# Two heads' scores as 64-row matmuls, weights kept split, and an order from a simulated list: an attention and two gated layers in one launch

## The chip, the cores and the metric

The kernel runs on one core of a Trainium2 chip. The metric is the time of one launch on the device in microseconds (us), as a median of runs. In the profile PE is TensorE (its weight loads are a row of their own, PEld), ACT is ScalarE, DVE is VectorE, POOL is GpSimd and SP is the engine that issues the DMAs.

## The reference

```python
# q, k, v: [4, 12, 448, 64] float32 (batch, heads, tokens, head size); weights are float64
scores = q @ k^T / sqrt(64) - log(448)
attn   = sigmoid(scores) @ v                       # -> x: [4 * 448 tokens, 12 * 64 = 768]
h = max(x @ w1, x @ w2, x @ w3);  y = h @ w_out    # all weights 768 x 768
g = y @ w_in;  out = (g * sigmoid(1.702 * g)) @ w_out2   # 768 x 2048, then 2048 x 768
```

## The kernel before

A block is one batch entry: 448 tokens, 12 heads (6 pairs), x of 6 tiles of 128 features. All matmuls have 448 columns. PE's float32r kind takes operands that were rounded, so a float32 number is split in an upper part (a rounded copy) and a lower part (the remainder, `rest`, a subtraction on DVE), and a product is made of three matmuls: upper x upper, upper x lower, lower x upper (`product`, L206). For a tile of 768 x 128 weights that is 18 matmuls, a unit.

*Attention.* A head's q and k lie in one tile `qkf` of 128 rows: both stand twice, in rows 0 to 63 and again in 64 to 127. The upper rows of q get its upper part, the lower rows its lower part, so one 128-row matmul with k's upper part on both halves gives two of the three products (L332), and one with k's lower part the third (L333). Scores of a head are made in chunks of 128 keys; the last 64 keys share a chunk. ScalarE makes sigmoids out of PSUM (L350, up to 896 columns a time). For attn @ v sigmoid and v are split too, except for six pairs of heads (`PLAIN`), whose product is made in plain float32 (L391). In the split product (L401) the two parts of v lie side by side as 128 columns, so its lower half has to be added to the upper one (`fold`, L432, L435).

*Weights.* They come as float64, 768 KB a tile. The high words times 2^-112 are made on ScalarE (`wy`, L134); the upper three bits of the low word are made on ScalarE as an 8-bit number (L136); VectorE clamps, shifts left by 3 and joins the bits (L158 to L160), and the float32 is split (L128, and `rest` in `lower`). In the first block each of the 24 tiles of the first two layers is so converted, and its float32 is stored in DRAM (`kept`); the three later blocks load that and split it again. The 32 tiles of the last two layers are converted while those run.

*Stages.* Block 0's attention runs alone with some of the next one's heads (`alone`, 16 steps). Then for each block the 24 units of its first two layers run with the next block's attention beside them. y stays in SBUF in two parts, in the place of x. Last come 32 steps of the last two layers, 256 features of one block at a time: two products of 18, then six sums of six matmuls (L640 to L642), added up in SBUF (L647).

*Order.* It is written out by hand: each engine works its instructions in the order of emission. Lists say which rounding is VectorE's and which ScalarE's (`UPPER_DVE`, `QK_DVE`, ...), `AHEAD` how many weight tiles are ready, `SPREAD` how the attention's steps are spread over units, and `mixed` interleaves VectorE's operations. DMAs all go through SP's queue; a load whose buffer is about to come free is held back by `soon` until the step's end.

Of the kernel before, what the change touches and what calls it, by code (L numbers as in the profile page):

```python
# [21 lines left out]
KEYS = 512  # 448 keys, the last 64 of them twice  # L22
# [9 lines left out]
SPREAD = (24, 24, 23, 1)
# where among the operations beside a unit the unit before it is finished
LATE = (0.3, 1)
WHOLE = 4
# how many weight tiles are ready beside each unit of a block: beside the last block's more and more, and the first
# of the last two layers'
AHEAD = (B - 1) * [[n + 2 for n in range(NW1)]]
AHEAD.append([2, 3, 4, 5, 7, 9, 11, 13, *range(14, 22), 22, 23, 23, 24, 25, 25, 26, 26])
# what VectorE rounds, where ScalarE does the rest: halves of heads' sigmoids, heads' v, pairs' x, parts of h, weight  # L40
# tiles, heads' q and k
UPPER_DVE = (0, 2, 5, 6, 10, 11, 12, 13, 15, 16, 17, 19, 22, 24, 25, 26, 28, 36, 45, 50, 52, 53, 54)
V_DVE = (0, 2, 4, 6, 8, 9, 14, 19, 20, 21)
X_DVE = (11, 13)
H_DVE = (5, 6, 7, 8, 9)
W_DVE = (3, 21, 23)
QK_DVE = (1, 2, 3, 5, 7, 9, 10, 13, 25)
# a float64's low word times LOW, rounded or cut off, is its upper 3 bits as a number of at most 7
LOW = 0.93 * 2.0**-29
# the largest value the weights' exponent shift leaves within float32  # L50
TOP = struct.unpack("f", struct.pack("I", (255 << 20) - (1 << 9)))[0]


def moe_chain_kernel(tc, qk, vv, v4, wa, wb, out):
    nc = tc.nc
    act, dve, pe, sp = nc.scalar, nc.vector, nc.tensor, nc.sync
    scale = 1.0 / math.sqrt(D)
# [6 lines left out]
    def rest(out_, in_, hi):
        dve.tensor_tensor(out_, in_, hi, op=ALU.subtract)  # L65

    def parts(p, name, shape):
        return [p.tile(shape, F32R, name=f"{name}{c}") for c in "hl"]

    def mixed(a, b, c=(), at=()):  # L70
        """VectorE's next operations: those of a and b in turn, and those of c where at says"""
        n, m = len(a), len(b)
        order = [((i + 0.5) / n, 1, f) for i, f in enumerate(a)] + [((i + 0.5) / m, 2, f) for i, f in enumerate(b)]
        order += [(x, 0, f) for x, f in zip(at, c)]
        for _, _, f in sorted(order, key=lambda x: x[:2]):
            f()
# [15 lines left out]
    pav_pool = pool("pav", bufs=2, space=PSUM)
    psc_pool = pool("psc", bufs=2, space=PSUM)
    psc1_pool = pool("psc1", bufs=1, space=PSUM)
    pav1_pool = pool("pav1", bufs=1, space=PSUM)
# [6 lines left out]
    seq = [("new", wa[i], kept[i]) for i in range(NW1)] + (B - 1) * [("kept", kept[i], None) for i in range(NW1)]  # L102
    seq += [("new", wb[i], None) for i in range(NW2)]
    news = [i for i, t in enumerate(seq) if t[0] == "new"]

    class Weights:
        def __init__(self):
            self.raw, self.y, self.c, self.hl = {}, {}, {}, {}
            self.i = -2
            self.free = [(n, wp) for n in range(3)]  # L110
            self.loads = 0

        def load(self, n):
            while self.loads < min(n, len(news)):
                i = news[self.loads]
                third = i < NW1 and i % 3 == 2
                t = (early if third else wp).tile(
                    [P, DM], mybir.dt.uint64, name="w64", tag="w64", bufs=1 if third else 2
                )
                sp.dma_start(t, seq[i][1])  # L120
                self.raw[i] = t
                self.loads += 1

        def upper(self, i):
            n, p = self.free.pop(0)
            h = p.tile([P, DM], F32R, name=f"wh{n}", tag=f"wh{n}", bufs=1)
            lo = p.tile([P, DM], F32R, name=f"wl{n}", tag=f"wl{n}", bufs=1)
            (dve.tensor_copy if i in W_DVE else act.copy)(h, self.c[i])  # L128
            self.hl[i] = (h, lo)
            self.free.append((n, p))  # L130

        def shift(self, i):
            y = self.y[i] = (early if i < NW1 else wp2).tile([P, DM], F32, name="wy", tag="wy", bufs=1)
            act.activation(y, self.words(i, F32, 1), AF.Copy, scale=2.0**-112)  # L134
# [3 lines left out]
        def words(self, i, dtype, n):  # L138
            return self.raw[i].bitcast(dtype).rearrange("p (n two) -> p n two", two=2)[:, :, n]

        def lower(self, i):
            c = self.c.pop(i)
            rest(self.hl[i][1], c, self.hl[i][0])
            if seq[i][2] is not None:
                soon(lambda: sp.dma_start(seq[i][2], c))

        def bits(self, i, halves):
            c = self.c[i] = wp.tile([P, DM], F32, name="wc", tag="wc", bufs=3)
            if seq[i][0] == "kept":
                sp.dma_start(c, seq[i][1])  # L150
                return []
            u, high, y = c.bitcast(U32), self.words(i, U32, 1), self.y.pop(i)
            del self.raw[i]
            n = i if i < NW1 else i - (B - 1) * NW1
            part = [slice(0, DM // 2), slice(DM // 2, DM)] if halves else [slice(0, DM)]

            todo = [
                lambda s: dve.tensor_scalar(c[:, s], y[:, s], -TOP, TOP, op0=ALU.max, op1=ALU.min),  # L158
                lambda s: dve.tensor_scalar(u[:, s], u[:, s], 3, None, op0=ALU.logical_shift_left),
                lambda s: dve.scalar_tensor_tensor(  # L160
                    u[:, s], high[:, s], 0x80000007, u[:, s], op0=ALU.bitwise_and, op1=ALU.bitwise_or
                ),
            ]
            todo = [lambda f=f, s=s: f(s) for f in todo for s in part]
            return todo + [lambda: soon(lambda: self.load(min(n + 4, max(NW1, n + 3))))]

        def step(self, halves=True):
            """the lower part of tile i, the bits of i + 2: gives what VectorE has to do"""
            i = self.i
            self.i += 1  # L170
            todo = []
            if B * NW1 <= i + 2 < len(seq):
# [564 lines left out]
```

## Time and profile before

| | |
|---|---|
| median of 3 runs | 1012.26 us (1009.37 to 1013.31) |
| profiled execution, its span | 1008.6 us, the time that the sums go by; the median is 3.7 above it |
| PE busy, matmul records | 990.7 us, 4774 |
| DVE busy | 663.4 us |
| ACT busy | 567.3 us |
| moved by DMA | 118.58 MB |

The span runs from the first to the last instruction. A matmul's record is longer than the distance to the next one, since matmuls are pipelined; the distance of two starts is what one takes. A plain float32 matmul leaves two records.

### The profile page before, as it was taken

What the parts mean: (1) busy time and instruction counts of PE and PEld (TensorE: products, weight loads), DVE (VectorE), ACT (ScalarE), POOL (GpSimd) and SP (SyncE); (2) the same over time, 40 slices, a digit from 0 to 9 for tenths busy, and PEclk for the clock granted to TensorE, in tenths of its full rate; (3) what the DMA queues carried; (4) which work ended last, traced back from release to release, by engine and by line L of the source; (5) the groups of instructions that cost most, each with busy time, mean ns of one, the idle gap of its engine ahead of it and who ended that gap; (6) DMA issues with size and microseconds to landing.
All of it is one profiled execution on the core that took longest, in us unless ns stands there. A gap on an engine that the chain in (4) does not pass through costs nothing.

```text
span 1008.6 us, 12335 instructions
## 1 busy us (share of the span) xinstructions
PE 990.7 (98%) x4774; PEld 898.4 (89%) x4774; DVE 663.4 (66%) x1125; ACT 567.3 (56%) x726; POOL 0.8 (0%) x6
## 2 busy tenths in 40 slices
PE   8999999899999999999999999999999999999998
PEld 6669888799999999999999899999999999999997
DVE  6888988897777877644465435665566666565544
ACT  5999999876676877533455655344334434443110
POOL 0000000000000000000000000000000000000000
PEclk9999999999999999999999999999999999999999
DMA  8686776663434343233522211111111111110023
GB/s 311 204 267 203 226 245 206 232 194 117 170 113 159 120 156 109 80 108 119 164 92 69 90 63 63 45 50 63 63 37 58 63 63 33 62 63 1 1 92 128
DMA packets 36059, 118.58 MB, mean 118 GB/s; under 512 B 4000, under 2 KB 7328, under 8 KB 36000
## 3 DMA queue, kind: packets, MB, share of 16 engines
q1 hardware_dynamic: 36000, 117.78, 35.3%
q8 instruction: 38, 0.62, 0.2%
q14 instruction: 21, 0.17, 0.1%
HBM read 102.83 MB, written 14.94 MB: 117 GB/s over the span
## 4 chain that ended last, share of the span: by engine, by line
PE 83%; ACT 10%; DVE 2%; issue 2%; DMA 1%; SPq 0%; DVEq 0%; ACTq 0%
PE pmm L212 17%; PE pmm L211 17%; PE pmm L210 17%; PE po L642 8%; PE po L641 7%; PE po L640 7%; PE pav L401 4%; PE psc L332 3%; PE psc L333 3%; ACT w L136 2%; ACT wy L134 2%; ACT a L350 2%; ACT wh L128 1%; PE pav L391 1%; ACT qkh L293 1%
## 5 line engine op out<-in xcount | busy, mean ns | idle before, releaser
L625 ACT ACTIVATE sg<-pmm 128x448 f32<-128x448 f32 x64 | 35.0, 547 | 218.8 <-PE pmm L212 218.8
L642 PE MATMUL po<-gh,wl 128*128 128x448 f32 x384 | 139.4, 363 | 0.0
L641 PE MATMUL po<-gl,wh 128*128 128x448 f32 x384 | 139.4, 363 | 0.0
L640 PE MATMUL po<-gh,wh 128*128 128x448 f32 x384 | 138.6, 361 | 0.6 <-ACT acc L644 0.6
L647 DVE TENSOR_TENSOR acc<-po,acc 128x448 f32<-128x448 f32 (+1 forms) x169 | 102.3, 619 | 52.0 <-PE po L642 50.0
L65 DVE TENSOR_TENSOR wl<-wc,wh 128x768 fp32r<-128x768 f32 x128 | 121.2, 952 | 4.7 <-ACT wh L128 3.7
L128 ACT CAST wh<-wc 128x768 fp32r<-128x768 f32 x125 | 106.8, 854 | 14.2 <-PE pmm L211 7.4
L136 ACT ACTIVATE w<-w 128x768 uint8<-128x768 uint32 x56 | 109.4, 1953 | 1.8
L350 ACT ACTIVATE a<-psc,bias 128x896 f32<-128x896 f32 x96 | 88.3, 961 | 26.6 <-PE psc L333 17.1
L627 DVE TENSOR_TENSOR gf<-pmm,sg 128x448 f32<-128x448 f32 x64 | 40.0, 625 | 86.0 <-ACT sg L625 85.7
L332 PE MATMUL psc<-qkh 128*128 128x448 f32 x192 | 74.8, 390 | 7.8 <-DVE qkh L65 4.7
L65 DVE TENSOR_TENSOR al<-a,ah 128x896 fp32r<-128x896 f32 x72 | 62.0, 892 | 24.7 <-ACT ah L358 24.6
L210 PE MATMUL pmm<-x0h,wh 128*128 128x448 f32 x204 | 75.5, 370 | 2.2 <-ACT mx L222 1.3
L640 PEld LDWEIGHTS po<-gh,wh 128*128 128x128 f32 x384 | 71.8, 187 | 6.2 <-ACT acc L644 1.0
L641 PEld LDWEIGHTS po<-gl,wh 128*128 128x128 f32 x384 | 72.1, 188 | 5.6
L642 PEld LDWEIGHTS po<-gh,wl 128*128 128x128 f32 x384 | 72.0, 188 | 4.0
L210 PE MATMUL pmm<-x1h,wh 128*128 128x448 f32 x204 | 74.7, 366 | 0.0
L210 PE MATMUL pmm<-x2h,wh 128*128 128x448 f32 x204 | 74.7, 366 | 0.0
L211 PE MATMUL pmm<-x1l,wh 128*128 128x448 f32 x204 | 74.6, 366 | 0.0
L211 PE MATMUL pmm<-x2l,wh 128*128 128x448 f32 x204 | 74.6, 366 | 0.0
L212 PE MATMUL pmm<-x1h,wl 128*128 128x448 f32 x204 | 74.6, 366 | 0.0
L212 PE MATMUL pmm<-x2h,wl 128*128 128x448 f32 x204 | 74.6, 365 | 0.0
(91 smaller groups left out, 2052.0 us busy)
## 6 DMA issues: line engine op xcount, KB each, us to landing
wc<-kept SPq DMA_DIRECT2D x72, 384.0 KB, 3.7
w<-in_wb SPq DMA_DIRECT2D x32, 768.0 KB, 4.2
qkf<-in_qk SPq DMA_DIRECT2D x47, 480.0 KB, 4.0
w<-in_wa SPq DMA_DIRECT2D x24, 768.0 KB, 6.7
kept<-wc SPq DMA_DIRECT2D x24, 384.0 KB, 6.7
out_t<-acc SPq DMA_DIRECT2D x23, 224.0 KB, 2.0
vf<-in_vv SPq DMA_DIRECT2D x18, 256.0 KB, 4.3
v<-in_v SPq DMA_DIRECT2D x6, 352.0 KB, 3.5
```

Source lines behind the costliest of these rows:

```text
L65: dve.tensor_tensor(out_, in_, hi, op=ALU.subtract)
L128: (dve.tensor_copy if i in W_DVE else act.copy)(h, self.c[i])
L136: act.activation(low, self.words(i, U32, 0), AF.Copy, scale=LOW)
L210: pe.matmul(ps, wh, xh, start=(k == 0), stop=False)
L211: pe.matmul(ps, wh, xl, start=False, stop=False)
L212: pe.matmul(ps, wl, xh, start=False, stop=(k == KC - 1))
L332: pe.matmul(ps, kh[:, c], qs, start=start, stop=False)
L350: act.activation(a, ps, AF.Sigmoid, bias=bias, scale=scale)
L640: pe.matmul(ps, wh[:, c], gh[:, j, :], start=(j == 0), stop=False)
L641: pe.matmul(ps, wh[:, c], gl[:, j, :], start=False, stop=False)
L642: pe.matmul(ps, wl[:, c], gh[:, j, :], start=False, stop=(j == 1))
L647: dve.tensor_tensor(ACC[b][:, o, h], ps[:, h], ACC[b][:, o, h], op=ALU.add)
```

## The change

One pair of heads takes the place of one head: q of both heads in rows 0 to 63 and 64 to 127, and k too, so a chunk of 128 keys takes three 64-row matmuls per head; those of the two heads use different rows of PE and different PSUM banks and stand next to each other in the order. The last 64 keys of both heads lie as a block diagonal, and take three 128-row matmuls for the pair. In the split pairs, attn @ v's last 64 keys are 64-row matmuls too. q and k are split once per pair, in two tiles of 960 columns.

A weight tile's three low bits come from one 16-bit shift on VectorE, in place, where ScalarE made an 8-bit number. A converted tile is kept in DRAM as its two parts (768 KB), and later blocks load both. y of each block goes to DRAM in two parts and is loaded again for the last two layers.

The order of emission comes from a simulation: every operation is recorded with the parts that it reads and writes, the engines that can do it and an assumed duration (a matmul 0.201 us, a pair of 64-row ones counted once); due times are worked out backwards, and a list schedule lets each engine take the ready operation with the earliest due time. Rings of buffers (`t`, `qh`, `ql` 2 each, weights of the first two layers 5, of the last two 7) replace the pools. Buffers of the last layers are allocated behind two gates: `to_late` when the attention is over, `to_acc` when the first two layers are.

```diff
-    def scores(ps, g, c, start=True, stop=True):
-        kh, kl, qs = qks[g]
-        pe.matmul(ps, kh[:, c], qs, start=start, stop=False)
-        pe.matmul(ps, kl[:, c], qs, start=False, stop=stop)
...
+        def score(self, c):
+            pair = c < 3
...
+                for n, (kx, qx) in enumerate(((h, h), (h, l), (l, h))):
+                    how = dict(start=n == 0, stop=n == 2)
+                    keys = slice(S + c * P, S + (c + 1) * P)
+                    for e in range(2 if pair else 0):
+                        r = slice(e * D, (e + 1) * D)
+                        pe.matmul(o[:, e, :], kx[r, keys], qx[r, :S], **how)
+                    if not pair:
+                        pe.matmul(o, kx[:, keys], qx[:, :S], **how)
...
+            O.pe(f, 3 * MM, [x[i] for x in (self.hi, self.lo) for i in used], [ps])
...
+            def parts(_):
+                v = self.vt()
+                for n, x in enumerate(a):
+                    for e in range(2):
+                        if c < 3:
+                            w = v[:, 2 * c + e].rearrange("p t d -> p (t d)")
+                            pe.matmul(av[e](), w, x()[:, e, :], start=c + n == 0, stop=False)
+                        else:
+                            r = slice(e * D, (e + 1) * D)
+                            w = v[r, 6].rearrange("p t d -> p (t d)")
+                            pe.matmul(av[e](), w, x()[r, :], start=False, stop=n == 1)
...
-            low = self.raw[i].bitcast(U8).rearrange("p (n eight) -> p n eight", eight=8)[:, :, 4]
-            act.activation(low, self.words(i, U32, 0), AF.Copy, scale=LOW)
...
+            lambda: dve.tensor_scalar(half(2), half(1), 13, None, op0=ALU.logical_shift_right),
...
+    def weights1(b, i):
+        hi, lo, t = split(w1s)
+        if b == 0:
+            new_weights(wa[i], hi, lo)
+            dma(kept[i], t, 768, [hi, lo], [kept[i]])
+        else:
+            dma(t, kept[i], 768, [kept[i]], [hi, lo])
+        return hi, lo
...
+    def unit2(b, m):
+        w, ps = weights1(b, 3 * KC + m), bank(mms)
+        product(ps, w, list(HS))
+        hi, lo, t = split(yst)
+        copy(hi, ps, S, psum=True)
+        rest(lo, ps, hi, S)
+        dma(ykept[b][m], t, 448, [hi, lo], [ykept[b][m]])
...
+        def offer(o):
+            for e in o.on:
+                heapq.heappush(ready[e], (o.late + (SLACK if e == "DVE" and len(o.on) > 1 else 0.0), o.n, o))
...
+            for e in free:
+                while free[e] <= now + 1e-9 and ready[e]:
+                    _, _, o = heapq.heappop(ready[e])
+                    if o in done:
+                        continue
+                    done.add(o)
+                    o.fn(e)
...
+    def step(p, c):
+        if p < NP:
+            if c == 0:
+                pairs[p] = Pair(p)
+            pairs[p].score(c)
+        if p > 0:
+            pairs[p - 1].weigh(c)
```

## Rows read from the trace of the kernel before

**Rows 1.** The page's first part: busy time, share, instructions of PE, PEld, DVE, ACT, POOL.
```profile
PE 990.7 (98%) x4774; PEld 898.4 (89%) x4774; DVE 663.4 (66%) x1125; ACT 567.3 (56%) x726; POOL 0.8 (0%) x6
```
**Rows 2.** Windows: stretch, length, busy us (records) per engine, clock, DMA share, GB/s.
```profile
0.00:20.00 20.00, 16.24 (x53) 12.60 (x54) 11.57 (x21) 10.83 (x13) 0.81 (x6) 0.91 0.90 328
0.00:200.00 200.00, 186.33 (x800) 152.66 (x801) 167.64 (x287) 178.51 (x204) 0.81 (x6) 0.98 0.72 239
200.00:300.00 100.00, 100.00 (x490) 91.66 (x489) 80.19 (x120) 69.72 (x94) 0.00 (x0) 1.00 0.46 150
300.00:400.00 100.00, 100.00 (x493) 92.27 (x492) 76.43 (x109) 76.68 (x105) 0.00 (x0) 1.00 0.41 133
600.00:700.00 100.00, 100.00 (x498) 93.13 (x497) 58.74 (x113) 41.82 (x54) 0.00 (x0) 1.00 0.17 55
```
**Rows 3.** PE in order of time, first 80 us: start, duration, line, operands, count.
```profile
14.09 2.42 PE L391 MATMUL pav<-a,v 128*128 128x448 f32 x6
16.00 0.72 PE L332 MATMUL psc<-qkh 128*128 128x448 f32 x1
16.55 0.37 PE L333 MATMUL psc<-qkh,kl 128*128 128x448 f32 x1
...
43.47 0.47 PE L332 MATMUL psc<-qkh 128*128 128x448 f32 x1 [1.33 <-ACT a L350]
43.78 0.36 PE L333 MATMUL psc<-qkh,kl 128*128 128x448 f32 x1
...
74.58 0.36 PE L210 MATMUL pmm<-x0h,wh 128*128 128x448 f32 x1
...
78.23 0.57 PE L401 MATMUL pav<-ah,vs 128*128 128x448 f32 x2
```
**Rows 4.** All engines in order of time, the end: the last matmul.
```profile
1004.62 0.37 PE L642 MATMUL po<-gh,wl 128*128 128x448 f32 x1
```
**Rows 5.** Groups by line, PE: count, busy us, mean ns, idle before.
```profile
L332 PE MATMUL psc<-qkh 128*128 128x448 f32 x192 | 74.8, 390 | 7.8 <-DVE qkh L65 4.7 <-ACT a L350 3.1
L333 PE MATMUL psc<-qkh,kl 128*128 128x448 f32 x192 | 71.1, 370 | 0.0
```
**Rows 6.** PE's weight loads in order of time, after a wait.
```profile
43.47 0.19 PEld L332 LDWEIGHTS psc<-qkh 128*128 128x128 f32 x1 [1.70 <-ACT a L350]
43.58 0.19 PEld L333 LDWEIGHTS psc<-qkh,kl 128*128 128x128 f32 x1
```
**Rows 7.** Groups by line and shape, DVE.
```profile
L65 DVE TENSOR_TENSOR wl<-wc,wh 128x768 fp32r<-128x768 f32 x128 | 121.2, 952 | 4.7 <-ACT wh L128 3.7
...
L65 DVE TENSOR_TENSOR al<-a,ah 128x896 fp32r<-128x896 f32 x42 | 45.4, 1088 | 24.7 <-ACT ah L358 24.6
...
L65 DVE TENSOR_TENSOR kl<-qkf,qkh 128x512 fp32r<-128x512 f32 x47 | 32.3, 687 | 6.7 <-ACT qkh L293 6.4
...
L65 DVE TENSOR_TENSOR qkh<-qkf,qkh 64x448 fp32r<-64x448 f32 x48 | 29.9, 622 | 0.9
...
L160 DVE SCALAR_TENSOR_TENSOR wc<-w,wc 128x768 uint32<-128x768 uint32 x13 | 12.4, 953 | 0.2
L159 DVE TENSOR_SCALAR wc<-wc 128x768 uint32<-128x768 uint32 x13 | 7.2, 556 | 0.2
```
**Rows 8.** Groups by line and shape, ACT.
```profile
L136 ACT ACTIVATE w<-w 128x768 uint8<-128x768 uint32 x56 | 109.4, 1953 | 1.8
L128 ACT CAST wh<-wc 128x768 fp32r<-128x768 f32 x125 | 106.8, 854 | 14.2 <-PE pmm L211 7.4 <-DMA wc<-kept 6.6
L350 ACT ACTIVATE a<-psc,bias 128x896 f32<-128x896 f32 x84 | 82.1, 1009 | 26.6 <-PE psc L333 17.1 <-DVE al L65 9.3
L358 ACT CAST ah<-a 128x896 fp32r<-128x896 f32 x57 | 51.5, 947 | 0.0
L134 ACT ACTIVATE wy<-w 128x768 f32<-128x768 f32 x56 | 50.9, 908 | 1.1 <-DVE wc L158 1.1
L293 ACT CAST qkh<-qkf 128x960 fp32r<-128x960 f32 x38 | 37.9, 996 | 0.1
```
**Rows 9.** DMA issues: count, KB each, median us from issue to landing.
```profile
wc<-kept SPq DMA_DIRECT2D x72, 384.0 KB, 3.7
...
out_t<-acc SPq DMA_DIRECT2D x23, 224.0 KB, 2.0
```

More of the change, by code (lines that the diff above doesn't have):

```diff
@@ L28 @@
 PLAIN = (0, 2, 3, 5, 6, 10)
-SPLIT = tuple(p for p in range(2 * NPAIR) if p not in PLAIN)
-EARLY = (6, 7, 11, 13, 15)
 WARM = 10
[L32 to L45, printed above, removed]
@@ new lines, with __init__, __call__, part @@
+class Tile:
+    def __init__(self, ring=None, get=None):
+        self.ring, self.get, self.ap, self.ops = ring, get, None, []
+    def __call__(self):
+        if self.ap is None:
+            self.ap = self.ring.make() if self.ring else self.get()
+        return self.ap
+    def part(self, cut=None):
+        return Part(self, cut)
+class Part:
+    def __init__(self, tile, cut):
+        self.tile, self.cut, self.writers, self.readers = tile, cut, [], []
+    def __call__(self):
+        ap = self.tile()
+        return self.cut(ap) if self.cut else ap
@@ L57, in moe_chain_kernel, with pool @@
     scale = 1.0 / math.sqrt(D)
-    def pool(name, bufs=1, side=None, **kw):
-        if side is not None:
-            kw["side"] = side
+    O = Order()
+    def pool(name, bufs=1, **kw):
         return tc.alloc_tile_pool(name=name, bufs=bufs, **kw)
[L64 to L76, printed above, removed]
@@ L92, in moe_chain_kernel @@
[L92 to L118, printed above, removed]
-                )
[L120 to L134, printed above, removed]
-            low = self.raw[i].bitcast(U8).rearrange("p (n eight) -> p n eight", eight=8)[:, :, 4]
-            act.activation(low, self.words(i, U32, 0), AF.Copy, scale=LOW)
[L138 to L172, printed above, removed]
-                self.shift(i + 2)
-            if 0 <= i < len(seq):
-                todo.append(lambda: self.lower(i))
-            if 0 <= i + 2 < len(seq):
-                todo += self.bits(i + 2, halves)
-            return todo
-        def ahead(self):
-            i = self.i
-            if 0 <= i < len(seq):
-                self.upper(i)
-            if i + 2 < NW1:
-                self.shift(i + 2)
-        def upto(self, i):
-            while self.i <= min(i, len(seq) - 1):
-                mixed(self.step(), [])
-                flush()
-                self.ahead()
@@ L194, in moe_chain_kernel @@
-    W = Weights()
-    waiting = []
-    def soon(f):
-        waiting.append(f)
-    def flush():
-        while waiting:
-            waiting.pop(0)()
-    def product(ps, w, x):
-        for k in range(KC):
-            wh, wl = (t[:, k * P : (k + 1) * P] for t in w)
-            xh, xl = (t[:, k, :] for t in x)
-            pe.matmul(ps, wh, xh, start=(k == 0), stop=False)
-            pe.matmul(ps, wh, xl, start=False, stop=False)
-            pe.matmul(ps, wl, xh, start=False, stop=(k == KC - 1))
@@ L495, in finish @@
-    def finish(g):
-        if g < NH and g % 2 == 0:
-            values(g)
-        h = g - 2
-        if 0 <= h < NH and not shared(h):
-            fold(h)
-        elif 0 <= h < NH and h % 2 == 1 and plain(h):
-            xf[h // 2] = products.pop(h - 1)
-            x_part(h // 2)
-        elif 0 <= h < NH and h % 2 == 1:
-            fold(h - 1)
-            fold(h)
-    def alone(g):
-        w = weigh(g - 2) if g >= 2 else iter(())
-        first(g)
-        score(g, 0)
-        score(g, 1)
-        next(w, 0)
-        next(w, 0)
-        steps = W.step(False) if g in EARLY else []
-        todo = splits(g) + sums(g)
-        between(g)
-        finish(g)
-        mixed(todo, steps)
-        flush()
-        if g < 3:
-            W.load(g + 1)
-        if g in EARLY or g + 1 == EARLY[0]:
-            W.ahead()
@@ L527, in between @@
-    def between(g):
-        if g % 2 == 1 and g >= 5 and not plain(g - 5):
-            x_part((g - 5) // 2)
-        if g + 2 < NH and g + 2 not in QK_DVE:
-            operands(g + 2)
-    def half(g, n):
-        if n == 0:
-            first(g)
-            if g < NH:
-                score(g, 0)
-                score(g, 1)
-            between(g)
-            return splits(g)
-        if 0 <= g - 2 < NH:
-            for _ in weigh(g - 2):
-                pass
-        todo = sums(g)
-        finish(g)
-        return todo
@@ new lines, in copy, with two, rest @@
+    def copy(to, of, n, psum=False, both=True):
+        engines = {"ACT": t_act(n)}
+        if both:
+            engines["DVE"] = t_two(n) if psum else t_one(n)
+        return O.op(engines, lambda e: (act.copy if e == "ACT" else dve.tensor_copy)(to(), of()), [of], [to])
+    def two(to, a, b, op, n):
+        return on("DVE", t_two(n), lambda: dve.tensor_tensor(to(), a(), b(), op=op), [a, b], [to])
+    def rest(to, of, hi, n):
+        return two(to, of, hi, ALU.subtract, n)
+    base = [pool("base", side="left")]
@@ new lines, in moe_chain_kernel, with banks @@
+    ts, his, los, a2s, a1s, ah2s, ah1s, al2s, al1s, vfs, vss, v4s, xfs, folds = att_rings
+    xs = [ring(xp, f"x{k}", [P, 2, S], 2, F32R) for k in range(KC)]
+    w1s = ring(xp, "w1", [P, 2, DM], 5, F32R)
+    hs = [ring(mid, f"h{k}", [P, 2, S], 1, F32R) for k in range(KC)]
+    mxs = ring(mid, "mx", [P, S], 2)
+    yst = ring(mid, "yst", [P, 2, S], 2, F32R)
+    def banks(p, name, n, shape=(P, 512)):
+        return O.ring(n, lambda: p[0].tile(list(shape), F32, name=name, tag=name, bufs=n))
+    scs, avs, mms = banks(patt, "sc", 2, (P, 2, 512)), banks(patt, "av", 2), banks(pmm, "mm", 2)
@@ new lines, in moe_chain_kernel @@
+    pos = banks(pout, "po", 6)
+    w2s = ring(late, "w2", [P, 2, DM], 7, F32R)
+    z0s = [ring(late, f"z{k}", [P, 2, S], 1, F32R) for k in range(KC)]
+    zs = [ring(acc, f"z{k}", [P, 2, S], B - 1, F32R) for k in range(KC)]
+    gs = ring(late, "g", [P, 2, 2, S], 2, F32R)
+    sgs = ring(late, "sg", [P, S], 2)
+    gfs = ring(late, "gf", [P, S], 2)
+    accs = ring(acc, "acc", [P, S], B * KC)
+    bias = base[0].tile([P, 1], F32, name="bias")
+    nc.gpsimd.memset(bias, -math.log(S))
+    warm = yst.tile().part()
@@ new lines, in moe_chain_kernel, with dram, bank @@
+    O.op({"-": 0.0}, lambda e: nc.gpsimd.memset(warm().bitcast(F32), 0.0), [], [warm])
+    warmed = base[0].tile([P, 1], F32, name="warmed")
+    act.activation(warmed, bias, AF.Sigmoid)
+    def dram(name, shape):
+        return Tile(get=lambda: scratch.tile(shape, F32R, name=name)).part()
+    kept = [dram(f"kept{i}", [P, 2, DM]) for i in range(NW1)]
+    ykept = [[dram(f"yk{b}_{k}", [P, 2, S]) for k in range(KC)] for b in range(B)]
+    def bank(r):
+        return r.tile().part(lambda a: a[:, :S])
@@ new lines, in split, with words, new_weights @@
+    def split(r):
+        t = r.tile()
+        return t.part(lambda a: a[:, 0]), t.part(lambda a: a[:, 1]), t
+    def words(a, dtype, n):
+        per = 8 // mybir.dt.size(dtype)
+        return a.bitcast(dtype).rearrange("p (n k) -> p n k", k=per)[:, :, n]
+    def new_weights(of, hi, lo):
+        raw, y = raws.tile().part(), ys.tile().part()
+        O.op({"SP": 768 / 330.0}, lambda e: sp.dma_start(raw(), of), (), [raw])
+        half = lambda n: words(raw(), U16, n)
+        u = lambda: y().bitcast(U32)
+        by = dict(op0=ALU.bitwise_and, op1=ALU.bitwise_or)
+        on("ACT", t_act(DM), lambda: act.activation(y(), words(raw(), F32, 1), AF.Copy, scale=2.0**-112), [raw], [y])
+        on(
+            "DVE",
+            t_one(DM),
+            lambda: dve.tensor_scalar(half(2), half(1), 13, None, op0=ALU.logical_shift_right),
+            [raw],
+            [raw],
+        )
+        on("DVE", t_one(DM), lambda: dve.tensor_scalar(y(), y(), -TOP, TOP, op0=ALU.max, op1=ALU.min), [y], [y])
+        on("DVE", t_one(DM), lambda: dve.tensor_scalar(u(), u(), 3, None, op0=ALU.logical_shift_left), [y], [y])
+        on(
+            "DVE",
+            t_two(DM),
+            lambda: dve.scalar_tensor_tensor(u(), words(raw(), U32, 1), 0x80000007, u(), **by),
+            [y, raw],
+            [y],
+        )
+        copy(hi, y, DM)
+        rest(lo, y, hi, DM)
@@ new lines, in moe_chain_kernel, with unit1 @@
+    pairs = [None] * NP
+    def step(p, c):
[5 more added lines that the diff above has]
+            pairs[p - 1].weigh(c)
+    HS, mx = [None] * KC, [None]
+    def unit1(b, m, e):
+        w, ps = weights1(b, 3 * m + e), bank(mms)
+        product(ps, w, X[b])
+        if e == 0:
+            mx[0] = mxs.tile().part()
+            copy(mx[0], ps, S, psum=True)
+            return
+        two(mx[0], ps, mx[0], ALU.max, S)
+        if e == 2:
+            hi, lo, _ = split(hs[m])
+            copy(hi, mx[0], S)
+            rest(lo, mx[0], hi, S)
+            HS[m] = (hi, lo)
@@ L643, in unit4 @@
             if grp == 0:
-                act.copy(ACC[b][:, o, :], ps)
+                ACC[b, o] = accs.tile().part()
+                copy(ACC[b, o], ps, S, psum=True)
                 continue
-            for h in halves if u == NG * B - 1 and o == KC - 1 else [slice(0, S)]:
-                dve.tensor_tensor(ACC[b][:, o, h], ps[:, h], ACC[b][:, o, h], op=ALU.add)
-                if grp == NG - 1:
-                    sp.dma_start(out[o, :, b * S : (b + 1) * S][:, h], ACC[b][:, o, h])
-    halves = [slice(0, S // 2), slice(S // 2, S)]
@@ new lines, in moe_chain_kernel, with warming @@
+    mm_warm = bank(avs)
+    def warming(_):
+        for n in range(WARM):
+            pe.matmul(mm_warm(), warm()[:, 0, :P], warm()[:, 1], start=n == 0, stop=n == WARM - 1)
+    O.pe(warming, 3.7, [warm], [mm_warm])
+    steps = [(p, c) for p in range(NP + 1) for c in range(4)]
+    at = 4 * (NPAIR + 1)
+    for s in steps[:at]:
+        step(*s)
+    order = [(1, m, e) for m in range(KC) for e in range(3)] + [(2, m, 0) for m in range(KC)]
+    for b in range(B):
+        first = at
+        for n, (layer, m, e) in enumerate(order):
+            while b < B - 1 and at < min(len(steps), first + -(-24 * (n + 1) // 22), 28 + 24 * (b + 1)):
+                step(*steps[at])
+                at += 1
+            unit1(b, m, e) if layer == 1 else unit2(b, m)
@@ L653, in moe_chain_kernel @@
+    first_ops = {o for r in (*att_rings, scs, avs) for t in r.tiles for o in t.ops}
+    gate = O.op({"-": 0.0}, to_late, after=first_ops)
+    for r in (w2s, *z0s, gs, sgs, gfs, pos):
+        r.gate = gate
     unit3(0)
[L654 removed]
     for u in range(NG * B):
[L656 removed]
         if u + 1 < NG * B:
@@ L659, in moe_chain_kernel @@
         unit4(u)
-    for p in (gp_, acc_pool, wp2, late, wp, low, pout_pool, pmm_pool, pav_pool, scratch):
-        p.release()
+    first_ops = {o for r in (*xs, w1s, *hs, mxs, yst) for t in r.tiles for o in t.ops}
+    gate = O.op({"-": 0.0}, to_acc, after=first_ops)
+    for r in (accs, *zs):
+        r.gate = gate
+    O.run()
+    for p in (late, base, acc, pout, pmm):
+        p[0].release()
+    scratch.release()
 def _bits(w):
```

644 lines of the change are left out of this document (293 added, 351 removed).

## The prediction

> **What bounds the kernel now.** I read the share of busy time first [rows 1]: the matrix engine (PE) is busy 98% of a span of 1008.6 us, VectorE (DVE) 66%, ScalarE (ACT) 56%. Busy time of PE is modelled, so I checked it by counting, in the windows [rows 2]. The reader is to see that from 200 us on, 490 to 498 matmuls of 448 columns stand in every 100 us: the engine takes one each 0.201 to 0.204 us whatever the others do. In the first 200 us only 800 records stand, beside DVE at 84% and ACT at 89%. The order in time [rows 3] gives the unit prices. A product of 18 matmuls runs from 74.58 to 78.23: 0.2028 each, called a slot below. A matmul in plain float32 leaves two records: six of them run from 14.09 to 16.35 (the next product's second matmul starts at 16.55, one slot later), 0.377 each, so about 0.75 for one such matmul. The first 200 us then hold 1.4 us before the first matmul, 4.1 us of warm-up, 84 float32 records x 0.375 = 31.5 and 706 slots x 0.203 = 143.3, in all 180.3; so PE stood still for 19.7 us. One such wait is the gap before 43.47 in [rows 3]. Later waits are about 1 us together. The span ends 4.0 us after the last matmul starts [rows 4]: an addition and the store. So a change can win in two places: fewer slots anywhere, or fewer waits in the first 200 us.
>
> **The change, part by part.** Sums are against the span of 1008.6; the median of the three runs lies 3.7 above it (their ends 0.8 and 4.7), which I add at the end.
>
> *Scores.* Before, a pair of heads takes 16 score matmuls (192 of either kind over 24 pairs [rows 5]). After, each of three chunks takes three pairs of 64-row matmuls, one for either head, and the last chunk three whole ones: 12 slots if the two halves of a pair run at once. That removes 4 x 24 = 96 slots. In attn @ v each of the six split pairs of the first two blocks falls from 16 to 14 slots (the last 64 keys of either head as 64-row matmuls), again if halves run at once: 12 slots. Together 108 x 0.203 = -21.9 us.
>
> *What a pair of 64-row matmuls takes.* No row shows one: every matmul of this trace uses 128 rows. There are 24 x 9 + 18 x 2 = 252 such pairs. Below, a pair costs one slot (0.203), above, two (0.406, the sum +51). Each half loads its own weights. After a wait, two weight loads start at 43.47 and 43.58 [rows 6], 0.11 apart, while the second matmul follows 0.31 after the first load: so a load occupies about 0.105 and is hidden otherwise. Two loads make 0.21, hardly more than a slot, so I take 0.21: 252 x 0.007 = +1.8.
>
> *Going from whole to halved array and back.* Each group of 64-row matmuls lies between whole ones: 72 score groups and 18 in attn @ v, at most 180 changes. The nearest row is the change between plain float32 and the rounded kind around 14.09 to 16.55, and it costs nothing that can be seen. The other bound is a change that empties the pipeline: the next weight load uncovered (0.105) and the tail of a matmul beyond its slot (0.36 recorded less 0.20), 0.265 in all, +48 us. I take 0 by the nearest row, and keep 48 for the range and as a rival.
>
> *Work of ACT and DVE in the first 200 us.* Prices are from [rows 7, 8]. q and k are split once for two heads: before 2 x (0.996 copy + 0.687 + 0.622), after one copy of 960 columns (0.996) and one remainder of 960, which I put at 1.16 from 0.687 at 512 and 0.952 at 768: 4.6 falls to 2.2 per pair. A split pair then holds sigmoids 3 x 1.01 + 0.63, upper parts 3 x 0.95 + 0.6, remainders 3 x 1.09 + 0.62, and about 4.6 for v, sums and x (eight operations of 448 columns, some 0.6 each): some 17.8 us of engine time (20.3 before), a plain pair 7.0 (9.4). A new weight tile lost the 1.953 on ACT and gained a 16-bit shift on DVE. Its price isn't shown: 0.555 if it goes like the shift of whole words, 0.953 if like the operation with a strided operand; I take 0.555, the row of the same kind of operation, the rest being +9.6 us of DVE over 24 tiles. A tile is 0.91 + 3 x 0.555 + 0.953 + 0.952 + 0.854 = 5.3, against 0.91 + 1.95 + 0.854 + 2 x 0.556 + 0.953 + 0.952 = 6.7. Up to the end of block 0 that is 6 x 7.0 + 6 x 17.8 + 14 for the pair begun + 24 x 5.3 + 25 for block 0's own results (42 such operations) = 315 us for two engines. Before, these two were busy 346 of 400 us in the first 200 [rows 2], 87%. At that share 315 us need 181. PE's own work to that point is 49.3 for the seven pairs ahead (5.5 start, 84 + 28 slots, 28 float32 matmuls) plus 124.2 for block 0 beside six pairs (432 + 72 + 56 slots, 14 float32 matmuls) = 173.5. So some 8 us of waiting stay, and a few for what an automatic order doesn't foresee: 12 in place of 20.3, -8.3 us. Cover for the shift is DVE's own slack; if it's gone, each further us on DVE there is one on PE.
>
> *Split weights and y through memory.* A tile of the first two layers is reloaded as both parts (768 KB for 384), so blocks 1 to 3 no longer split 72 tiles; that work (0.854 + 0.952 each) lay beside PE and brings nothing by itself. Its price is traffic. Up to the end of block 0: 24 x 1536 KB of weights in and out, 13 x 480 of q and k, 3.7 MB of v and 2.7 MB of y, about 50 MB; at the 328 GB/s that the first 20 us reach [rows 2] that is 154 us of some 187: near the edge, but covered. In blocks 1 to 3 traffic rises from about 125 to some 225 GB/s (per block 18.9 MB of weights, 4.3 of q, k and v, 2.8 of y in 117 us). It stays under 328, so no load is late with five tiles of buffer, 18 us ahead. But slots grow with traffic: 493 matmuls in 100 us at 133 GB/s, 498 at 55 [rows 2], which is 0.0020 us for 78 GB/s; 100 GB/s more is 0.0026 x 1600 slots = +4 us (0 if it was the attention beside them and not the traffic).
>
> *Going to the last two layers.* y of blocks 1 to 3 gets its buffers only when the last y of block 3 is stored. Copy and remainder (1.2), store and first load (about 3.5 each, by the landing times of 224 and 384 KB [rows 9]), and six loads of 1.4 put block 1's y some 15 us after PE's last product there. PE has block 0's two products (7.3) and its six sums (7.3) to do meanwhile: 14.6. I count +1.5 (0 to 8, the latter if the sums aren't drawn forward).
>
> *Order.* A simulated list order replaces the written one; its effect is in the 12 us above. Lists of SP's queue are in simulated order too, so a load can stand behind a store that waits; with two or more buffers in every ring I count that at nothing, and the bound from the trace is the old waiting, 20.
>
> Sum: 1008.6 - 21.9 + 1.8 - 8.3 + 4 + 1.5 = 985.7, and with 3.7 around it **989 us**. Its own range is 970 (no waits at all in the first 200 us, no traffic cost) to 1003.
>
> **Rivals.**
> *The change of shape drains PE.* Mechanism: at each of 180 changes PE waits for its pipeline and loads weights uncovered. The place is every score step, and it decides from (1012.3 - 989) / 180 = 0.13 us per change; at 0.265 the time is 989 + 48 = 1037, slower. For it: a wait in the trace always leaves an uncovered load. Against: the float32 change costs nothing. The Trainium skill ("TensorEngine Tiling (Array Packing)", Key Properties) says that changing the tiling mode, not just the tile, drains TensorE; no run here shows it, and by that rule this rival is the likely one. I give it 0.18, spread from 1005 to 1037.
>
> *Halves don't run at once* (the change doesn't do what it says): 252 more slots, 989 + 49 = 1038. For it: no row shows two matmuls at once. Against: loads aren't the limit. The skill ("TensorE: Matmul & The Clock Gate", Part 3) has matmuls on different row groups start about 4 ns apart; that would put the pair at 0.207 and take 0.8 us off the sum. I give it 0.06.
>
> *Supply rules the first 190 us.* The shift at 0.953 (+9.6 on DVE), DMA at 83% of the best rate with stores among the loads, and an order made with wrong prices: the waits are 35 in place of 12, 1012. For it: ACT and DVE are already at 84 and 89% there. Against: each pair and tile needs less of both. 0.20, from 1003 to 1018.
>
> *No waits and no traffic cost*: about 970, 0.04.
>
> **How the numbers follow.** Forecast 0.52. A measurement of this kernel can tell about 0.5% from no change, 1007.2 to 1017.3 being the same. Faster: 0.52 + 0.04 + 0.09 of the supply case + 0.02 of the draining one = 0.67. Same: 0.08 + 0.04 = 0.12. Slower: the rest, 0.21. The range for 8 in 10 is 968 to 1024: outside lie most of the case of halves one by one and the upper third of draining.
>
> **What would show it.** In the order in time after: two 64-row matmuls of one pair starting within 0.02 us and the next pair 0.20 to 0.22 later (right), or 0.4 later (halves one by one). The gap between the last 64-row matmul and the next whole one: a slot, or up to 0.27 more. The first product of block 0 should start near 57 us (74.58 before), block 1's near 190. In blocks 1 to 3 matmuls per 100 us should fall by no more than two per cent against the last stage. The 16-bit shift's mean duration decides between 0.55 and 0.95. The prediction is wrong if PE waits over 25 us in all, or if a score step of six takes over 0.75 us.

## The result, and the profile after

After the change the kernel takes 1016.44 us (median of 4 runs, 1015.61 to 1017.1) against 1011.68 for the one before beside it: ratio 1.0054 [1.0036, 1.0072]. It is slower by half a per cent, and the forecast was 2.3% faster. The profiled execution's span is 1013.8 us against 1008.6.

The page's first part after, columns as in [rows 1]:
```profile
PE 998.4 (98%) x4918; PEld 864.8 (85%) x4918; DVE 619.5 (61%) x936; ACT 360.5 (36%) x523; POOL 1.1 (0%) x6
```
DVE and ACT lost 44 and 207 us, as meant, and PE's share is what it was. Only the weight loads hint at something: there are more of them, yet they are busy 4 points less.

The windows after, columns as in [rows 2]:
```profile
0.00:200.00 200.00, 190.73 (x915) 141.26 (x916) 173.03 (x244) 136.19 (x181) 1.08 (x6) 1.00 0.78 279
200.00:300.00 100.00, 99.16 (x513) 82.23 (x512) 61.27 (x90) 46.28 (x64) 0.00 (x0) 1.00 0.64 229
300.00:400.00 100.00, 100.00 (x509) 83.85 (x508) 50.77 (x72) 42.01 (x60) 0.00 (x0) 1.00 0.58 193
600.00:700.00 100.00, 100.00 (x492) 91.99 (x491) 63.32 (x102) 23.08 (x38) 0.00 (x0) 1.00 0.14 48
700.00:800.00 100.00, 100.00 (x492) 92.15 (x491) 71.71 (x115) 22.08 (x35) 0.00 (x0) 1.00 0.18 64
```
From 200 to 400 us a pair of 64-row matmuls is two records, so the larger counts say nothing of speed; but PEld fell from about 92 to 83 us in 100. From 600 us on only whole matmuls run, and there are fewer of them: 492 where [rows 2] has 498. For 700 to 800 us the window before was:
```profile
700.00:800.00 100.00, 100.00 (x499) 93.12 (x497) 61.98 (x118) 39.19 (x49) 0.00 (x0) 1.00 0.15 49
```
A busy PE hides both losses. Marks in PE's order of time show where they fall: the first product of block 0, the first of the last two layers, and the last matmul. Before, the first and the last are 74.58 [rows 3] and 1004.62 [rows 4], and the middle one is
```profile
539.71 0.36 PE L210 MATMUL pmm<-x0h,wh 128*128 128x448 f32 x1
```
After:
```profile
65.40 0.37 PE L363 MATMUL mm<-x,w 128*128 128x448 f32 x1
537.51 0.37 PE L363 MATMUL mm<-z,w 128*128 128x448 f32 x1
1009.61 0.37 PE L555 MATMUL po<-g,w 128*128 128x448 f32 x1
```
The attention that runs alone gained 9.2 us. Blocks 0 to 3 took 472.1 in place of 465.1, +7.0, where the forecast had a gain. By count PE has 13.8 us less to do ahead of block 0 (124 slots and 56 float32 records, 166 and 70 before, warm-up left out) and 8.1 us less in the blocks (2144 and 28, 2210 and 14 before): the first stage gave two thirds of that, the blocks lost 15 us against it. The last two layers took 472.1 in place of 464.9, +7.2, although no product there is changed. The tail adds 0.1; in all +5.1.

**A group of 64-row matmuls.** PE in order of time after, once among whole score matmuls and products (x2 is both halves of a pair):
```profile
252.31 0.36 PE L414 MATMUL sc<-ql,qh 128*128 128x448 f32 x1
252.51 0.37 PE L414 MATMUL sc<-qh,ql 128*128 128x448 f32 x1
252.81 0.47 PE L450 MATMUL av<-ah,vs 64*128 64x448 f32 x2
253.12 0.36 PE L450 MATMUL av<-al,vs 64*128 64x448 f32 x2
253.41 0.47 PE L363 MATMUL mm<-x,w 128*128 128x448 f32 x1
253.72 0.36 PE L364 MATMUL mm<-x,w 128*128 128x448 f32 x1
```
and PE's weight loads beside them:
```profile
252.31 0.19 PEld L414 LDWEIGHTS sc<-qh,ql 128*128 128x128 f32 x1
252.81 0.19 PEld L450 LDWEIGHTS av<-ah,vs 64*128 64x128 f32 x2 [0.30 <-issue]
252.92 0.19 PEld L450 LDWEIGHTS av<-al,vs 64*128 64x128 f32 x2
253.41 0.19 PEld L363 LDWEIGHTS mm<-x,w 128*128 128x128 f32 x1 [0.30 <-issue]
253.52 0.19 PEld L364 LDWEIGHTS mm<-x,w 128*128 128x128 f32 x1
```
The steady distance of starts is 0.20. The first pair starts 0.30 after the last whole matmul: its load isn't made ahead, as the one at 252.31 was (its matmul starts at 252.51), but is recorded as starting with it. The next follows 0.31 later, one uncovered load more, as after a wait [rows 6]. Leaving the group costs the same (0.29 and 0.31). So each of the two changes costs about 0.09 + 0.105, and a group 0.385 (the 59 groups behind block 0's start have a median of 0.39). There are 78 groups (neighbours without a whole matmul between them are one): 78 x 0.385 = 30 us, against 21.9 saved. The Trainium skill ("TensorEngine Tiling (Array Packing)", Key Properties) says that changing the mode drains TensorE; the trace agrees, at 0.19 us a change, the uncovered load with it.

### The profile page after: what moved, and what is told of

Its sections match the earlier page's. It is cut to its first block, busy times and chain, and to the rows that moved or that the text cites. A ratio compares the mean times of both kernels' runs of the same rounds, so it can differ in the third digit from the quotient of the medians.

```text
span 1013.8 us, 12189 instructions
## 1 busy us (share of the span) xinstructions
PE 998.4 (98%) x4918; PEld 864.8 (85%) x4918; DVE 619.5 (61%) x936; ACT 360.5 (36%) x523; POOL 1.1 (0%) x6
## 4 chain that ended last, share of the span: by engine, by line
PE 97%; ACT 1%; DMA 1%; DVE 0%; issue 0%; SPq 0%; DVEq 0%; ACTq 0%
PE mm L363 19%; PE mm L365 19%; PE mm L364 19%; PE po L554 8%; PE po L555 8%; PE po L553 8%; PE av L446 5%; PE sc L412 5%; PE av L438 3%; PE sc L414 1%; PE av L450 1%; ACT a L419 1%; DMA v<-in_v 1%; DMA t<-in_qk 0%; ACT fold L470 0%
## 5 line engine op out<-in xcount | busy, mean ns | idle before, releaser
L363 PE MATMUL mm<-x,w 128*128 128x448 f32 x432 | 161.0, 373 | 0.0
L364 PE MATMUL mm<-x,w 128*128 128x448 f32 x432 | 157.8, 365 | 0.0
L365 PE MATMUL mm<-x,w 128*128 128x448 f32 x432 | 157.6, 365 | 0.0
L553 PE MATMUL po<-g,w 128*128 128x448 f32 x384 | 140.4, 366 | 1.3 <-ACT g L217 1.3
L365 PE MATMUL mm<-z,w 128*128 128x448 f32 x384 | 141.4, 368 | 0.0
L363 PE MATMUL mm<-z,w 128*128 128x448 f32 x384 | 141.3, 368 | 0.0
L364 PE MATMUL mm<-z,w 128*128 128x448 f32 x384 | 141.2, 368 | 0.0
L554 PE MATMUL po<-g,w 128*128 128x448 f32 x384 | 140.4, 366 | 0.2 <-DVE g L220 0.2
L555 PE MATMUL po<-g,w 128*128 128x448 f32 x384 | 140.1, 365 | 0.0
L537 ACT ACTIVATE sg<-mm 128x448 f32<-128x448 f32 x64 | 34.8, 544 | 258.6 <-PE mm L365 258.6
L419 ACT ACTIVATE a<-sc,bias 128x896 f32<-128x896 f32 (+1 forms) x96 | 87.3, 915 | 93.3 <-PE sc L412 68.0
L220 DVE TENSOR_TENSOR al<-a,ah 128x896 fp32r<-128x896 f32 (+1 forms) x72 | 69.7, 974 | 49.2 <-ACT ah L217 48.8
L220 DVE TENSOR_TENSOR gf<-mm,sg 128x448 f32<-128x448 f32 x64 | 39.9, 624 | 97.0 <-ACT sg L537 96.5
L363 PEld LDWEIGHTS mm<-x,w 128*128 128x128 f32 x432 | 81.1, 188 | 10.7 <-issue 3.3
L364 PEld LDWEIGHTS mm<-x,w 128*128 128x128 f32 x432 | 81.2, 188 | 7.3 <-issue 1.1
L365 PEld LDWEIGHTS mm<-x,w 128*128 128x128 f32 x432 | 81.1, 188 | 6.4
L553 PEld LDWEIGHTS po<-g,w 128*128 128x128 f32 x384 | 72.1, 188 | 7.5 <-ACT g L217 1.6
L365 PEld LDWEIGHTS mm<-z,w 128*128 128x128 f32 x384 | 72.2, 188 | 6.8
L364 PEld LDWEIGHTS mm<-z,w 128*128 128x128 f32 x384 | 72.2, 188 | 6.7
L363 PEld LDWEIGHTS mm<-z,w 128*128 128x128 f32 x384 | 72.2, 188 | 6.6
L554 PEld LDWEIGHTS po<-g,w 128*128 128x128 f32 x384 | 72.1, 188 | 6.2 <-DVE g L220 0.5
```

The lines of the kernel that those rows point to most:

```text
L220: return on("DVE", t_two(n), lambda: dve.tensor_tensor(to(), a(), b(), op=op), [a, b], [to])
L363: pe.matmul(ps(), wh[:, c], xh, start=k == 0, stop=False)
L364: pe.matmul(ps(), wh[:, c], xl, start=False, stop=False)
L365: pe.matmul(ps(), wl[:, c], xh, start=False, stop=k == KC - 1)
L419: on("ACT", t_act(n) + 0.07, lambda: act.activation(a(), ps(), AF.Sigmoid, bias=bias, scale=scale), [ps], [a])
L537: on("ACT", t_act(S), lambda sg=sg, ps=ps: act.activation(sg(), ps(), AF.Sigmoid, scale=1.702), [ps], [sg])
```

## Experiments

Theory A: the changes of shape take what the slots give. Theory B: they only fill time in which PE would wait anyway, and something else costs. Theory C: the two halves don't run at once. The edits are shortened to the lines that matter. Line numbers in a row are those of its own kernel.

**One whole matmul for each pair of halves (e1).** As many slots, no change of shape.
```diff
- pe.matmul(o[:, e, :], kx[r, keys], qx[r, :S], **how)   # e = 0, 1
+ pe.matmul(o[:, n > 0, :], kx[:, keys], qx[:, :S], start=n < 2, stop=n != 1)
  # last keys of attn @ v: one whole matmul where two 64-row ones ran
```


> The changed kernel with one whole 128-row matmul in place of each pair of 64-row ones (252 of them), so PE has as many slots and no change of shape; this mixes the two heads' products and leaves half of them out. Theory A (each of 78 groups of 64-row matmuls costs 0.385 us: 0.09 to empty and 0.105 of uncovered weight load, on either side): 1016.4 - 30 = 986 us, ratio to the kernel before about 0.975. Rival B (the changes only fill time in which PE would wait for sigmoids and weight tiles anyway): no more than 8 us gained, 1008 to 1016. Rival C (the two halves don't really run at once): a whole matmul for each pair would save 0.2 each, -50 us, 966.

992.37 us, ratio 0.9828 [0.981, 0.9845], span 988.9: 24.9 of the 30 us are back. Its marks, and the window that answers to [rows 2] at 300 us:
```profile
62.82 0.36 PE L363 MATMUL mm<-x,w 128*128 128x448 f32 x1
512.69 0.37 PE L363 MATMUL mm<-z,w 128*128 128x448 f32 x1
984.79 0.37 PE L554 MATMUL po<-g,w 128*128 128x448 f32 x1
```
```profile
300.00:400.00 100.00, 100.00 (x495) 92.47 (x494) 52.15 (x76) 43.94 (x58) 0.00 (x0) 1.00 0.57 195
```
The 59 groups after block 0's start are priced at 59 x 0.385 = 22.7 and gave back 472.1 - 449.9 = 22.2. The 19 before it are priced at 7.3 and gave back 2.6: there PE waits some 1.6 us more, for ACT and a load of v, and its granted clock was 0.97 over the stretch (1.00 after), worth just under 2. A fits. The halves cost no second slot, and no cost of traffic shows: 495 whole matmuls at 195 GB/s, 493 at 133 before.

**Fewer groups, the same work (e2).** 46 groups in place of 78.
```diff
+ if c == 0: s.score((0, 1))                        # chunks 0 and 1 in a row
+ if c == 1: w.weigh(0); w.weigh(1)
+ if c == 2: w.weigh(2); s.score((2,), w.weigh(3, True)); w.finish()
+ if c == 3: s.score((3,))
```


> The changed kernel with the same matmuls in fewer groups: chunks 0 and 1 of a pair's scores stand together, chunk 2 behind the pair before's last 64-row products. 78 groups become 46, nothing else. Theory A: 32 x 0.385 = -12.3 us, 1004 (ratio 0.993), if no new waits come in the first 60 us, where two score chunks now need both PSUM buffers at once (up to +4). Rival B: 1014 to 1018, no gain.

1005.66 us, ratio 0.996 [0.9949, 0.997], span 1003.7: 10.1 less than after, where 32 x 0.385 = 12.3 was priced. The 6 groups fewer before block 0 brought nothing (it starts at 66.97); blocks 0 to 3 take 460.5, 11.6 less, where 26 groups fewer are priced at 10.0. A group in order of time:
```profile
225.15 0.36 PE L365 MATMUL mm<-x,w 128*128 128x448 f32 x1
225.44 0.47 PE L466 MATMUL av<-ah,vs 64*128 64x448 f32 x2
225.75 0.37 PE L466 MATMUL av<-al,vs 64*128 64x448 f32 x2
225.96 0.37 PE L413 MATMUL sc<-qh 64*128 64x448 f32 x2
226.16 0.37 PE L413 MATMUL sc<-ql,qh 64*128 64x448 f32 x2
226.37 0.37 PE L413 MATMUL sc<-qh,ql 64*128 64x448 f32 x2
226.66 0.47 PE L415 MATMUL sc<-qh 128*128 128x448 f32 x1
226.97 0.36 PE L415 MATMUL sc<-ql,qh 128*128 128x448 f32 x1
```
Inside it, after its first pair, a pair takes 0.20 to 0.21, whichever operation it belongs to; only the edges cost.

**More groups, the same work (e3).** 215 groups: products with v between the pairs.
```diff
+ if other: other[0](n)      # after each of the three pairs of a score step
```


> The changed kernel with the same matmuls in more groups: between the three pairs of a score step stand matmuls of the pair before's product with v. 78 groups become 215. Theory A: 137 x 0.385 = +52.7 us, 1069 (ratio 1.057). Rival B: under +10 us in the part where units of the first two layers stand beside, 1016 to 1026.

1082.55 us, ratio 1.0718 [1.0677, 1.0759], 13.5 more than A's 1069. Blocks 0 to 3 take 520.1 between the marks, +48; 109 groups more are priced at 42. The start is later by 24.3 us, more than 28 groups (10.8) explain; there the granted clock was 0.78 of 2.4 GHz over 70 us, and 0.50, the lower level of 1.2 GHz, from 25 to 48 us:
```profile
0.00:70.00 70.00, 62.65 (x176) 28.05 (x176) 43.56 (x62) 38.35 (x50) 1.08 (x6) 0.78 0.64 221
25.00:48.00 23.00, 22.11 (x50) 9.27 (x51) 11.69 (x17) 7.47 (x11) 0.00 (x0) 0.50 0.47 155
```
At 0.78, some 15 of the 70 us are lost, which with the 10.8 covers the 24.3. The four runs had mean clocks of 0.983 to 0.996 and spans of 1086.0 to 1075.2; span times clock is 1067 to 1072 in each, an estimate of the span at full clock, 54 to 58 above after, where A priced 52.7. Why the clock was low isn't shown. With e2 the time goes with the number of groups in both directions.

**The old sixteen score matmuls in the new kernel (e7).**
```diff
+ for n, (kx, qx) in enumerate(((h, h), (h, l), (l, h), (l, h))):
+     pe.matmul(o[:, n // 2, :], kx[:, keys], qx[:, :S], start=n % 2 == 0, stop=n % 2 == 1)
```


> The changed kernel with 16 whole score matmuls per pair of heads, as many as before, and no 64-row matmul (attn @ v's last keys as many as before too): the rest of the change without its new scores; this mixes the two heads' products. Theory A: 1016.4 - 30 + 21.9 = 1008 us, so the rest of the change is worth some 3 us against the kernel before (ratio 0.997): waits 9 less, 6 lost by slower slots in the last two layers. Rival B: at 21.9 more slots it is slower than the changed kernel, 1020 or more.

1007.52 us, ratio 0.9979 [0.9969, 0.9989], span 1005.6. The rest of the change (kept weights, list order, shift) is worth 0.2%, with the 7.2 us lost in the last two layers in it; the 64-row scores turn that into a loss.

**The 16-bit shift left out (e9).**
```diff
- lambda: dve.tensor_scalar(half(2), half(1), 13, None, op0=ALU.logical_shift_right)
```


> The changed kernel without the 16-bit shift, so that the weights' low three bits are left out. Its 56 instructions took 1.04 us each, not the 0.555 counted. Theory A (PE and the changes of shape are the bound, the shift lies beside PE): at most 3 us gained, 1013 to 1017. Rival F (VectorE is the bound in the first 200 us, where 24 of them are 25 us of its time): 8 us or more gained, under 1008.

1015.58 us, ratio 1.0058 [1.0045, 1.0071], as after. Groups by line after, DVE; the first is the shift, the third the shift of whole words ([rows 7] has 556):
```profile
L327 DVE TENSOR_SCALAR raw<-raw 128x768 uint16<-128x768 uint16 x56 | 58.1, 1038 | 0.0
L336 DVE SCALAR_TENSOR_TENSOR y<-raw,y 128x768 uint32<-128x768 uint32 x56 | 52.8, 952 | 0.3
L332 DVE TENSOR_SCALAR y<-y 128x768 uint32<-128x768 uint32 x56 | 32.6, 582 | 0.0
```
The shift is dearer than both my bounds, and hidden all the same.

**The last two layers.** The mean slot there grew, waits left out, from about 0.2015 to 0.2041, and the products differ: 0.2027 for those on block 0's z (z is y, loaded again) in seven of its eight units, 0.2064 for the other three blocks' (0.2067 in the first unit of all, block 0's). In PE's order of time after, 36 matmuls on block 0's z, 36 with w_out2 (`po`), and 36 on another block's z:
```profile
708.68 0.36 PE L363 MATMUL mm<-z,w 128*128 128x448 f32 x1
...
715.98 0.36 PE L553 MATMUL po<-g,w 128*128 128x448 f32 x1
...
723.27 0.37 PE L363 MATMUL mm<-z,w 128*128 128x448 f32 x1
...
730.70 0.36 PE L553 MATMUL po<-g,w 128*128 128x448 f32 x1
```
What differs between them is where the tiles begin in SBUF. Before, the starts of moving operand and weights lay 64 bytes apart (modulo 128) for w_out2's products (0.2003) and 0 for x (0.2027); after, 0 for w_out2 (0.2027) and block 0's z (0.2027), 32 for the other z (0.2064). These distances are worked out from the sizes of the tiles in their order of allocation; no trace shows an address. Theory D: this distance sets the slot, and 64 is best. Theory E or G: it doesn't.

The kernel after with distance 64 everywhere (e4):
```diff
+ w1s = shifted(xp, "w1", [P, 2, DM], 5, F32R, 64)       # begins 64 bytes in
+ w2s = shifted(late, "w2", [P, 2, DM], 7, F32R, 64)
+ zs = [shifted(acc, f"z{k}", [P, 2, S], B - 1, F32R, 96) for k in range(KC)]
```


> The changed kernel with its weight tiles begun 64 bytes later and the y tiles of the last two layers 96 bytes later, nothing else: in each unit the moving operand then begins 64 bytes (of 128) from the weights; before, 0, and 32 for three of four blocks in the last two layers. Theory D (a slot depends on where the two operands begin: 0.2002 us at a distance of 64, 0.2025 at 0, 0.2064 at 32): 864 slots x 0.0062 + 3168 x 0.0023 = -12.7 us, 1004 (ratio 0.993). Rival E (slots are longer in the last stage because of the new loads or the order): no change, 1014 to 1018.

1008.77 us, ratio 0.9985 [0.9974, 0.9996], span 1005.9: 7.9 less than after, where D asked 12.7; the last two layers take 466.7 us, 5.4 less.

The kernel before with x tiles 64 bytes later (e5):
```diff
- return [p.tile(shape, F32R, name=f"{name}{c}") for c in "hl"]
+ ts = [p.tile([shape[0], n + 32], F32R, name=f"{name}{c}") for c in "hl"]
+ return [t[:, 16 : 16 + n].rearrange("p (i j) -> p i j", i=shape[1]) for t in ts]   # not for h
```


> The kernel before with the tiles of x begun 64 bytes later, so that the 2448 matmuls on x have a distance of 64 in place of 0 bytes (of 128) to the weights. Theory D: 1296 x 0.003 + 1152 x 0.0022 = -6.4 us, ratio 0.994. Rival E: no change, ratio 0.999 to 1.001.

1006.36 us, ratio 0.9976 [0.9964, 0.9988]: 2.4 us by the ratio, less than half of the 6.4 that D asked. The last two layers gain 2.7 us, where D asked 2.5 (1152 x 0.0022); blocks 0 to 3 gain 0.6, where it asked 3.9.

e2 with distance 32 (e10) and 96 (e11) everywhere, by the same helper with 96 / 96 / 96 and 32 / 32 / 96 bytes:

> The kernel with 46 groups, its weight and y tiles moved so that in every unit the moving operand begins 32 bytes (of 128) from the weights. Theory D (a slot of 0.206 at a distance of 32, as three of four blocks showed): against the version with 46 groups and unmoved tiles 3168 slots x 0.0039 = +12 us, 1018 (ratio 1.008). Rival G (it isn't the distance but where those y tiles alone lie): 1000 to 1008.

> The same with a distance of 96 bytes in every unit. No unit of the other runs had it. Theory D, if only the distance's size counts (96 is 32 the other way round): as with 32, 1018 (ratio 1.008). If 64 is the one distance that helps and the rest are as 0: 1006 (ratio 0.996).

1005.71 us, ratio 0.9964 [0.9953, 0.9976], and 1007.25, ratio 0.998 [0.997, 0.999]. The windows from 700 us of e4, e5, e10 and e11, in this order:
```profile
700.00:800.00 100.00, 100.00 (x498) 93.12 (x497) 69.03 (x111) 22.18 (x35) 0.00 (x0) 1.00 0.18 64
```
```profile
700.00:800.00 100.00, 100.00 (x502) 93.69 (x501) 62.33 (x119) 38.50 (x48) 0.00 (x0) 1.00 0.17 56
```
```profile
700.00:800.00 100.00, 100.00 (x491) 91.85 (x490) 68.21 (x109) 21.60 (x35) 0.00 (x0) 1.00 0.18 64
```
```profile
700.00:800.00 100.00, 100.00 (x490) 91.70 (x489) 67.70 (x109) 21.90 (x35) 0.00 (x0) 1.00 0.18 64
```
At 64 there are 498 and 502 matmuls, at 32 and 96 491 and 490, about as many as after, with its mixed distances, has (492). So the start of a tile matters: moving tiles alone gave back 5.4 of the 7.2 us lost in the last stage (e4). But D's figures fell: distance 32 gives about 0.204, not 0.2064, and e10 is no slower than e2 (1005.66), where D asked 12 us more; 64 gives 0.2013 to 0.2021 in e4, not 0.2002. Block 0's first unit, at a distance of 0 like its other seven, doesn't fit D either. What else enters stays open.

**Both cures together (e6).** e2 with e4's starts.

> The changed kernel with 46 groups of 64-row matmuls in place of 78 and with the weight and y tiles begun at a distance of 64 bytes. Both theories together: 1016.4 - 10 (as measured for the groups) - 12.7 = 994 us, ratio 0.984. If the two don't add (the shorter slots only let PE wait longer), 1000 or more.

994.78 us (994.53 to 998.43), ratio 0.9862 [0.9849, 0.9875], span 992.9, 20.9 below after's (e2 alone 10.1, e4 alone 7.9): it beats both kernels with all of the work. Its marks:
```profile
66.17 0.37 PE L375 MATMUL mm<-x,w 128*128 128x448 f32 x1
522.05 0.36 PE L375 MATMUL mm<-z,w 128*128 128x448 f32 x1
988.71 0.37 PE L600 MATMUL po<-g,w 128*128 128x448 f32 x1
```

## Why the prediction was wrong

**Change of shape: the step that failed.** "I take 0 by the nearest row" stood for up to 180 changes. The row, from plain float32 to the rounded kind, leaves the array whole and doesn't bear on it. The runs show 0.19 per change, 156 changes, 30 us; in e1 24.9 of them were on the path. The upper bound (an uncovered load and a tail, 0.265) was the better guide, and the rival decided from 0.13, as it said. It had 0.18 where it should have led. Its time, 1037, was too high because groups merge and a change costs less than the bound. A score step of six, from its first pair to the next whole matmul, takes 0.79, over the 0.75 that the prediction named as its sign of being wrong. That 1016.4 lies between 968 and 1024 is owed to the rivals, this one above all, that had widened the range; the forecast's own, 970 to 1003, misses it.

**Slots and pairs: right, where PE is the bound.** Two halves start 0.003 us apart (median) and the next pair 0.20 later, so the halves run at once; 0.21 was near. e7 and e1 have no 64-row matmul and differ by the 108 slots: in blocks 0 to 3 the 72 of them are 14.6 us and bring 13.6 (463.5 to 449.9). The 36 ahead of block 0 are 7.3 and bring 3.1 (65.87 to 62.82), since PE waits there and e1's clock was 0.97. In all 16.7 of the 21.9 come.

**Waits in the first 200 us: right in sign, half in size.** The first product of block 0 starts at 65.40, not near 57, and block 1's at 200.18 (214.39 before), not near 190. In e1, without groups, block 0 still starts at 62.82, 5.8 after 57: 2.4 because the scores of eight pairs stand ahead of it and not of seven, just under 2 by e1's clock, the rest supply. PE's gaps between starts, above 0.12 us beyond a slot and without the warm-up, fall from 18.9 to 12.2 us in all. Of the 18.9 about 2.9 are no waits but slots at the lower clock, which the prediction took for PE standing still, though its own row has 0.98 for the 200 us. There are two such stretches of some 3.4 us; a window in the second, before:
```profile
196.90:200.20 3.30, 3.30 (x10) 2.90 (x10) 3.24 (x6) 2.45 (x3) 0.00 (x0) 0.50 0.19 80
```
So the waits fell by about 4 in place of 8.3. Those that are named after are short and scattered; columns: line, what it waited for, us in total, times, longest:
```profile
PE sc L412 <- ACT a L419: 5.6, 6, 1.4
PE av L438 <- DMA v<-in_v: 1.8, 1, 1.8
PE av L582 <- POOL yst L290: 1.7, 1, 1.7
PE po L553 <- ACT g L217: 1.3, 1, 1.3
```
The last of them is the passage to the last two layers: 1.3, near the +1.5 counted.

**Traffic: wrong, small.** +4 was counted and e1's window shows 0 (495 at 195 GB/s, 493 at 133): the slower slots of blocks 1 to 3 before don't look slow from traffic, the case that the step left open.

**The last two layers: not foreseen.** Apart from the passage they were taken as unchanged, a term at nothing. Longer slots there cost most of the +7.2 us: e4, which moves tiles alone, gives 5.4 back.

Together, from the forecast span of 985.7: +24.9 for the changes, -4 for traffic, -1.8 for the pairs (e1's 24.9 holds what they cost), +5.4 for the starts of tiles is 1010.2; the remaining 3.6 to 1013.8 is about what the waits didn't give. The sum is a rough one, since slots, waits and clock ahead of block 0 run into each other.

## What to carry to other kernels

Count how often TensorE changes between whole and 64-row matmuls, not only how many slots go: here a group cost 0.385 us, almost two slots, so by these figures one that saves a slot loses and one that saves four pays. When work is reordered, put 64-row matmuls in a row, across operations. A PE that is busy 98% can hide both: count starts, look at the weight loads' busy time, and compare stages that nothing was done to, since new buffers move the old ones.

## What the hardware showed unexpectedly

The same matmul of 448 columns took 0.2003 to 0.2064 us a slot in the last two layers before and after, 3% between the ends. Moving where its operands begin in SBUF, and nothing else, took the slot on z from 0.2056 to 0.2021 in the mean (e4) and that on x from 0.2027 to 0.2005 (e5). A 16-bit shift with a stride took 1038 ns for 768 elements, more than a two-operand operation on 32-bit words (952).
